# Repeating the queries of all batches on PE, with shared PSUM slots, split first loads and interleaved weights

## The chip, the cores and the metric

The kernel runs on one core of a Trainium2 chip. The metric is the device time of one execution in microseconds (us), and the median of several executions is quoted. The engines are PE (matmuls; PEld is its loading of weights), DVE (vector), ACT (scalar and activation), POOL (general) and SP, which here only issues DMA transfers. All quoted times come from the chip.

For a program on one core, a run is called slow when it is over 1.5% above the fastest run of the same kernel.

## The reference, cut to what matters

A polynomial-sketch attention over 4 batches, 4 heads, 1088 tokens and head size 32 feeds a feed-forward block with a squared relu:

```python
def phi(x):                                   # x: (batch, head, token, 32)
    a = einsum('rd,bhsd->bhsr', S1, x)        # 8 values
    b = einsum('rd,bhsd->bhsr', S2, x)        # 8 values
    return outer(a, b)                        # 64 features per token
q_p, k_p = phi(q), phi(k)
kv  = einsum('bhsf,bhsd->bhfd', k_p, v)       # one 64 x 32 matrix per head
z   = sum(k_p, axis=tokens)
x   = einsum('bhsf,bhfd->bhsd', q_p, kv) / (q_p @ z + 1e-6)
# x becomes 4352 tokens x 128
h = x @ w_in                                  # 128 -> 2048
out = relu(h) ** 2 @ w_out                    # 2048 -> 128
```

The disputed step is the product of query features. For every token the 8 values `a` and the 8 values `b` have to be spread over 64 partitions each before they can be multiplied element by element. This spreading is called "repetition" below.

## The kernel before: the parts that matter

The kernel describes its work as a graph of operations. Each one carries estimated costs for the engines that could run it. While the program is being built, a list scheduler picks an order, and the operations are then given to the engines in exactly that order. An engine takes its instructions in that order, so a wait in the middle of its list holds up everything behind it.

```python
G = Graph({"h": 2, "o": 1, "a": 3, "r": 4, "g": 4, "osb": 3})
h_t = [P(f"h{i}", [128, 1024]) for i in range(2)]     # PSUM, 1024 columns each
o_t = [P(f"o{i}", [128, 512]) for i in range(1)]
a_t = [P(f"a{i}", [128, 512]) for i in range(3)]      # for the attention
```

Batch 0 repeats its queries on PE: a matmul with a matrix that holds the sketch, repeated, writes the 64 copies directly. The others compute the sketch once (`qs`), and DMA makes the copies:

```python
if b == 0:
    for g in range(3):                                 # thirds of the tokens
        c0, n = 384 * g, 384 if g < 2 else 320
        # for x in (0, 1), for pr in (0, 1):
        nc.tensor.matmul(h_t[hb.slot][:, 512 * pr : 512 * pr + n],
                         SR[64 * pr : 64 * pr + 64, x].rearrange("p a x y -> p (a x y)"),
                         qT[i][64 * pr : 64 * pr + 64, c0 : c0 + n], start=True, stop=True)
        # ... ACT copies one factor to Ar, DVE multiplies the other by it
else:
    # ... qs = sketch of q (PE, ACT); bd = half of it written to DRAM
    reps.append(add(f"rb{b}.{pr}.{hp}", {"SP": (0.5, 4.0)}, f_rb, ...))   # Br <- bd, repeated
    reps.append(add(f"ra{b}.{ch}.{pr}", {"SP": (0.5, 4.0)}, f_ra, ...))   # Ar <- qs, repeated
    # ...
    o = add(f"qp{b}.{g}.{pr}", {"POOL": pool(n)}, f_qp, reps[...] + ...)  # qp = Ar * Br on POOL
# ... (cut)
o_num = add(f"num{b}.{g}", {"PE": pe(0.8)}, f_num, need + o_kve, vt(8 + g), alloc=[nb])
```

The pair `(0.5, 4.0)` is what the scheduler believes about one such transfer: 0.5 us to issue, landed 4.0 us after its start. The feed-forward block has two alternatives for the relu:

```python
o2 = add(f"r.{n}.{m}", {"ACT": act(W * N), "DVE": dve(W * N)}, f_r, [o1], p - 0.5, alloc=[rb], uses=[hb])
```

Of the kernel before, what the change touches and what calls it, by code (L numbers as in the profile page):

```python
# [16 lines left out]
LOOK = 0.12  # L17


class Buf:  # L20
    def __init__(self, kind):
        self.kind = kind
        self.users = []
        self.slot = None
        self.pending = 0


class Op:
    def __init__(self, name, alts, fn, deps, pri, alloc, uses, port):
        self.name, self.alts, self.fn, self.pri = name, alts, fn, pri  # L30
        self.deps = [d for d in deps if d is not None]
        self.alloc, self.uses, self.port = alloc, uses, port
        self.start = self.end = self.eng = None


class Graph:





# [4 lines left out]
    def add(self, name, alts, fn, deps=(), pri=0.0, alloc=(), uses=(), port=()):  # L46
        op = Op(name, alts, fn, deps, pri, list(alloc), list(alloc) + list(uses), port)
        for b in op.uses:
            b.users.append(op)
            b.pending += 1  # L50
        self.ops.append(op)
        return op

    def slot_time(self, kind):
        best = None
        for i, (t, b) in enumerate(self.slots[kind]):
            if b is not None and b.pending:
                continue
            if best is None or t < best[0]:
                best = (t, i)  # L60
        return best

    def run(self):
        eng_free, port_free = {}, 0.0
        todo = {id(o): len(o.deps) for o in self.ops}
        succ = {}
        for o in self.ops:
            for d in o.deps:
                succ.setdefault(id(d), []).append(o)
        ready = [o for o in self.ops if todo[id(o)] == 0]  # L70
        order = []
        while ready:
            cands = []
            for o in ready:
                t_slot = 0.0
                ok = True
                for b in o.alloc:
                    s = self.slot_time(b.kind)
                    if s is None:
                        ok = False  # L80
                        break
                    t_slot = max(t_slot, s[0] + SEM)
# [3 lines left out]
                for e, (busy, lat) in o.alts.items():  # L86
                    t = max(eng_free.get(e, 0.0), t_slot)
                    for d in o.deps:
                        t = max(t, d.end + (SEM if d.eng != e else 0.0))
                    if e in o.port:  # L90
                        t = max(t, port_free)
                    if best is None or t + lat < best[0]:
                        best = (t + lat, t, e, busy, lat)
# [4 lines left out]
                (c for c in cands if c[0] <= t0 + LOOK), key=lambda c: (c[1].pri, c[0]))  # L98
            for b in o.alloc:
                i = self.slot_time(b.kind)[1]  # L100
                b.slot = i
                self.slots[b.kind][i] = [t, b]
            o.start, o.end, o.eng = t, t + lat, e
            eng_free[e] = t + busy
            if e in o.port:
                port_free = t + busy
            for b in o.uses:
                b.pending -= 1
                sl = self.slots[b.kind][b.slot]
# [12 lines left out]
def act(n):  # L122
    return (0.833e-3 * n + 0.16, 0.833e-3 * n + 0.2)
# [6 lines left out]
def pool(n, rate=2.2e-3):  # L130
# [8 lines left out]
def kernel(  # L139
# [20 lines left out]
    HS = S // 2  # L160
# [3 lines left out]
    dr = ctx.enter_context(tc.tile_pool(name="dr", bufs=1, space=bass.MemoryType.DRAM))  # L164
# [8 lines left out]
    G = Graph({"h": 2, "o": 1, "a": 3, "r": 4, "g": 4, "osb": 3})  # L173
    h_t = [P(f"h{i}", [128, 1024]) for i in range(2)]
    o_t = [P(f"o{i}", [128, 512]) for i in range(1)]
    a_t = [P(f"a{i}", [128, 512]) for i in range(3)]
    r_t = [T(f"r{i}", [128, 1024], BF16) for i in range(4)]
    g_t = [T(f"g{i}", [128, 1024], BF16) for i in range(4)]
    osb_t = [T(f"osb{i}", [128, 512]) for i in range(3)]
# [5 lines left out]
    ST = T("ST", [128, 32])  # L185
    SK = T("SK", [128, 2, H, R])
# [4 lines left out]
    NB = 2  # L191
# [5 lines left out]
    vtl = [T(f"vtl{i}", [128, H, D]) for i in range(NB)]  # L197
# [4 lines left out]
    qs = [T(f"qs{i}", [128, HS]) for i in range(NB)]  # L202
    Ar = [T(f"Ar{i}", [128, 2, S]) for i in range(NB)]
    Br = [T(f"Br{i}", [128, 2, S]) for i in range(NB)]
    qp = [T(f"qp{i}", [128, 2, S]) for i in range(NB)]
    bd = [dr.tile([32, S], F32, name=f"bd{i}", tag=f"bd{i}") for i in range(NB)]
    den = [T(f"den{i}", [128, 12]) for i in range(NB)]
    rec = [T(f"rec{i}", [128, 12]) for i in range(NB)]
    xs = [T(f"xs{i}", [128, 3, 128], BF16) for i in range(NB)]

    add = G.add


    def f_S(eng):
        nc.vector.memset(S_sb, 0.0)
    o_S0 = add("S0", {"DVE": dve(32)}, f_S, pri=-100)

    def f_Sld(S, off):
        def f(eng):
            for h in range(H):  # L220
                nc.scalar.dma_start(out=S_sb[32 * h + off : 32 * h + off + R, :], in_=S)
        return f
    o_S1 = add("S1", {"ACT": (1.0, 3.0)}, f_Sld(S1, 0), [o_S0], -100)
    o_S2 = add("S2", {"ACT": (1.0, 3.0)}, f_Sld(S2, R), [o_S0], -100)
    o_SKz = add("SKz", {"DVE": dve(64)}, lambda e: nc.vector.memset(SK, 0.0), pri=-99)
    o_ST = add("ST", {"DVE": dve(32)}, lambda e: nc.vector.transpose(ST, S_sb), [o_S1, o_S2], -98)

    def f_SK(h):
        def f(eng):
            nc.vector.tensor_copy(  # L230
                SK[32 * h : 32 * h + 32, :, h, :],
                ST[32 * h : 32 * h + 32, 0 : 2 * R].rearrange("d (x r) -> d x r", x=2))
        return f
    o_SK = [add(f"SK{h}", {"DVE": dve(16)}, f_SK(h), [o_ST, o_SKz], -97) for h in range(H)]

    o_SRz = add("SRz", {"POOL": (0.4, 0.5)}, lambda e: nc.gpsimd.memset(SR, 0.0), pri=-99)
    o_SR = []
    for h in range(H):
        for x in range(2):
            def f(e, h=h, x=x):  # L240
                s = ST[32 * h : 32 * h + 32, R * x : R * x + R]
                s = s[:, None, :] if x else s[:, :, None]
                nc.gpsimd.tensor_copy(SR[32 * h : 32 * h + 32, x, h % 2], s.to_broadcast([32, R, R]))
            o_SR.append(add(f"SR{h}{x}", {"POOL": (0.2, 0.25)}, f, [o_ST, o_SRz], -96))

    o_iota = add("iota", {"POOL": (0.4, 0.5)}, lambda e: nc.gpsimd.iota(
        iot, pattern=[[1, 128]], base=0, channel_multiplier=-1), pri=-100)
    o_id = add("ident", {"DVE": dve(128)}, lambda e: nc.vector.tensor_single_scalar(
        ident, iot, 0, op=ALU.is_equal), [o_iota], 1)
    o_win = add("w_in", {"POOL": (1.2, 8.0)}, lambda e: nc.gpsimd.dma_start(  # L250
        out=w_in, in_=moe_w_in), pri=-99)
    o_wout = add("w_out", {"POOL": (1.2, 9.0)}, lambda e: nc.gpsimd.dma_start(
        out=w_out, in_=moe_w_out.rearrange("(ct c) d -> c ct d", c=128)), pri=-98)
    z_ops = {}
    for i in range(NB):
        def f_z(e, i=i):
            nc.gpsimd.memset(vp[i], 1.0)
            nc.gpsimd.memset(vp[i][64:128, :, NJ - 1, :], 0.0)
            nc.gpsimd.memset(kvz[i], 0.0)
        z_ops[i] = add(f"z{i}", {"POOL": (1.5, 1.6)}, f_z, pri=-97 + 50 * i)  # L260


# [6 lines left out]
    def attention(b, vt):  # L269
# [3 lines left out]
        def ld(dst, src, lo, hi):  # L273
            def f(e):
                nc.sync.dma_start(
                    out=dst[:, lo * D : hi * D],
                    in_=src[b].rearrange("h (t c) d -> (h t) (c d)", c=C)[:, lo * D : hi * D])
            return f
        parts = [(0, C)]
        o_k = add(f"ldk{b}", {"SP": (0.6, 3.4)}, ld(kin[i], k, 0, C), prev(b, "tk"), vt(0) - 30)  # L280
        o_q = add(f"ldq{b}", {"SP": (0.6, 3.4)}, ld(qin[i], q, 0, C), prev(b, "tq"), vt(0) - 29)
        o_v = []
        for g in range(4):
            def f(e, g=g):
                nc.sync.dma_start(
                    out=vin[i][32 * g : 32 * g + 32].rearrange("p h j d -> p h (j d)"),
                    in_=v[b].rearrange("h (t c) d -> t h c d", c=C)[:, :, 8 * g : 8 * g + 8, :].rearrange(
                        "t h c d -> t h (c d)"))
            o_v.append(add(f"ldv{b}.{g}", {"SP": (0.5, 3.0)}, f, prev(b, "vp"), vt(0) - 28))
        for g in range(2):  # L290
            def f(e, g=g):
                nc.sync.dma_start(
                    out=vtl[i][32 * g : 32 * g + 32],
                    in_=v[b].rearrange("h (t c) d -> t h c d", c=C)[:, :, 32 + g, :])
            o_v.append(add(f"ldv{b}.{4+g}", {"SP": (0.5, 3.0)}, f, prev(b, "vp"), vt(0) - 28))

        def f_vp(e):
            nc.gpsimd.tensor_copy(vp[i][:, :, 0:8, 0:D], vin[i])  # L298
            nc.gpsimd.tensor_copy(vp[i][0:64, :, 8, 0:D], vtl[i][0:64])
        o_vp = add(f"vp{b}", {"POOL": (1.6, 1.7)}, f_vp, o_v + [z_ops[i]] + prev(b, "kv"), vt(1))  # L300
        mine("vp", o_vp)


        kT3 = kT[i].rearrange("p (c t) -> p c t", t=32)
        prods = []
        for part, (j0, j1) in enumerate(((0, 4), (4, 9))):
            nj = j1 - j0

# [315 lines left out]
```

## Time and profile before

| Before, profiled run | |
|---|---|
| Median | 148.48 us |
| Span in the profile | 144.6 us |
| First feed-forward matmul | 27.8 us |
| PE stopped before numerator matmuls | 42.6 to 49.0 and 99.6 to 108.4 us |
| Time per chunk of 512 tokens at the end | 9.0 us |

The profile page of the kernel before gives busy time per engine, then rows of 40 equal slices of the span (3.6 us each) with the busy share in tenths. PEclk is the granted PE clock and DMA the busy share of the DMA engines, also in tenths:

```profile
PE 106.7 (74%) x1507; PEld 58.8 (41%) x1524; DVE 101.9 (70%) x192; ACT 67.7 (47%) x90; POOL 30.2 (21%) x48
...
PE   0008999799970496998999999995018898999850
...
PEclk9999999999999559999999999999555999999997
DMA  4999998788866687421300405896640003003042
...
L464 POOL TENSOR_TENSOR qp<-Ar,Br 128x384 f32<-128x384 f32 (+1 forms) x18 | 17.5, 998 | 54.7 <-DMA out_dram<-osb 36.7
L483 PE MATMUL a<-kvz,qp 128*32 128x66 f32 x576 | 13.8, 252 | 16.5 <-POOL qp L464 15.0
L539 DVE TENSOR_SCALAR r<-h 128x1024 bf16<-128x1024 f32 x13 | 15.8, 1218 | 3.6 <-PE h L531 3.6
```

No engine is busy throughout, and the average of 74% hides the interesting part. The PE row shows two holes, `04` and `01`, each with slices of about half rate in and behind it in the PEclk row. The groups (busy us, mean ns | idle before, releaser) name the waiter of the holes: the numerator matmuls L483 waited 15.0 us for POOL's product `qp`. The table by stages (window, length, busy us of each engine, granted clock, DMA share, GB/s) puts numbers on the holes:

```profile
42.60:49.00 6.40, 0.36 (x12) 0.20 (x14) 1.47 (x5) 0.39 (x1) 2.08 (x3) 0.85 0.65 177
49.00:55.00 6.00, 5.53 (x141) 3.94 (x146) 2.16 (x7) 0.55 (x2) 3.46 (x4) 0.59 0.81 141
99.60:108.40 8.80, 0.70 (x10) 0.20 (x8) 0.00 (x0) 0.62 (x1) 2.00 (x3) 0.62 0.52 153
118.00:140.00 22.00, 19.80 (x97) 9.20 (x95) 20.42 (x29) 14.40 (x15) 0.00 (x0) 1.00 0.18 31
```

In 15.2 us PE worked 1.06 us, and right after the first hole its clock was 0.59. The last row is the end, where only feed-forward is left: DVE is busy 20.42 of 22 us and ACT only 14.40, because DVE does the squares and also some of the relus (L539).

What did POOL wait for? The waits view of the kernel before says this (waiter, releaser: us, times, longest):

```profile
POOL qp L464 <- DMA out_dram<-osb: 36.7, 2, 34.4
...
PE a L483 <- POOL qp L464: 15.0, 6, 5.3
```

The first of these lines is a trap: a product of queries does not wait for a store of the output. The profile infers releasers from semaphores and names the one that came last. The chain of waits (start us, us, what) is the better witness for the first hole:

```profile
40.09 6.35 DMA Br<-bd
46.44 1.48 issue
47.91 1.00 POOL qp L464
48.96 1.33 PE a L483 x40
```

The repetition by DMA took 6.35 us where the scheduler's constant says 4.0. The scheduler had placed the numerators where it thought their data would be ready, and the feed-forward work behind them could not pass. For the second hole this view again names a store of the output. By the timeline, SP issued that batch's last copies `Ar` and `Br` only between 92.34 and 100.07 us, behind stores, and the first product on POOL ran at 104.10.

### The profile page before, as it was taken

To read this page: it belongs to the slowest core of one execution; us is meant where nothing else is said; L and a number is where in the kernel's file an instruction comes from. 1 tells how busy PE (TensorE), PEld (TensorE's weight loads), DVE (VectorE), ACT (ScalarE), POOL (GpSimd) and SP (SyncE) were. 2 spreads that over 40 slices of the span, in tenths; PEclk is the share of its full clock that TensorE was granted. 3 is DMA by queue.
4 is the path that set the end of the run, shared out by engine and by line. 5 is a ranking of instruction groups with operands and counts; after the bars stand their busy time and mean duration, and the time that the engine had idled before them with its cause. 6 is when DMAs were issued, how large, how long until landed. Compare 5 with 4: busy or idle time off the path is not lost.

```text
span 144.6 us, 3697 instructions
## 1 busy us (share of the span) xinstructions
PE 106.7 (74%) x1507; PEld 58.8 (41%) x1524; DVE 101.9 (70%) x192; ACT 67.7 (47%) x90; POOL 30.2 (21%) x48
## 2 busy tenths in 40 slices
PE   0008999799970496998999999995018898999850
PEld 0007477364520364565445437331006443333540
DVE  1219789898991038969999998693002999998960
ACT  0201331668580007643896896555000678377730
POOL 8308230300402750049200000000139000000000
PEclk9999999999999559999999999999555999999997
DMA  4999998788866687421300405896640003003042
GB/s 127 292 194 306 303 349 151 247 225 119 174 178 195 107 141 185 148 118 27 57 0 9 70 0 86 118 139 161 204 97 0 5 2 65 8 7 66 5 71 38
DMA packets 28017, 17.32 MB, mean 120 GB/s; under 512 B 22304, under 2 KB 24352, under 8 KB 28000
## 3 DMA queue, kind: packets, MB, share of 16 engines
q1 hardware_dynamic: 25664, 16.02, 47.2%
q0 software_dynamic: 2208, 1.05, 5.6%
q8 instruction: 12, 0.20, 0.5%
q10 hardware_dynamic: 128, 0.01, 0.1%
q14 instruction: 5, 0.04, 0.1%
HBM read 12.13 MB, written 2.65 MB: 102 GB/s over the span
## 4 chain that ended last, share of the span: by engine, by line
DVE 31%; PE 23%; SPq 15%; DMA 14%; issue 8%; POOL 1%; ACT 1%; POOLq 1%; DVEq 0%; ACTq 0%
DVE g L543 13%; SPq L451 7%; DMA S_sb<-in_S_dram 6%; PE o L550 6%; SPq L444 5%; PE h L531 5%; DMA Br<-bd 4%; DMA out_dram<-osb 4%; DVE r L539 4%; PE a L483 4%; SPq L566 3%; PE h L396 3%; DVE osb L557 3%; DVE xs L495 2%; PE a L359 2%
## 5 line engine op out<-in xcount | busy, mean ns | idle before, releaser
L537 ACT ACTIVATE r<-h 128x1024 bf16<-128x1024 f32 x55 | 54.6, 1023 | 21.7 <-PE h L531 16.2
L543 DVE TENSOR_TENSOR g<-r 128x1024 bf16<-128x1024 bf16 x68 | 45.2, 706 | 1.8 <-ACT r L537 1.1
L531 PE MATMUL h<-xT,w_in 128*128 128x512 bf16 (+1 forms) x135 | 38.8, 373 | 1.7 <-DVE r L539 0.4
L550 PE MATMUL o<-g,w_out 128*128 128x512 bf16 (+1 forms) x136 | 37.7, 367 | 2.5 <-DVE g L543 1.3
L464 POOL TENSOR_TENSOR qp<-Ar,Br 128x384 f32<-128x384 f32 (+1 forms) x18 | 17.5, 998 | 54.7 <-DMA out_dram<-osb 36.7
L483 PE MATMUL a<-kvz,qp 128*32 128x66 f32 x576 | 13.8, 252 | 16.5 <-POOL qp L464 15.0
L531 PEld LDWEIGHTS <-w_in 128*128 128x128 bf16 x144 | 13.5, 98 | 18.1 <-issue 5.0
L550 PEld LDWEIGHTS <-w_out 128*128 128x128 bf16 x144 | 12.8, 97 | 16.9 <-issue 7.2
L483 PEld LDWEIGHTS a<-kvz,qp 128*32 128x32 f32 x576 | 11.2, 128 | 20.8 <-POOL qp L464 17.8
L539 DVE TENSOR_SCALAR r<-h 128x1024 bf16<-128x1024 f32 x13 | 15.8, 1218 | 3.6 <-PE h L531 3.6
L493 DVE TENSOR_SCALAR den<-a 128x12 f32<-128x12 f32 x12 | 2.0, 164 | 20.6 <-PE a L483 20.6
L326 PE MATMUL a<-SK,kT 128*32 128x64 f32 x288 | 7.3, 251 | 11.5 <-DVE SK L230 11.5
L513 ACT COPY xT<-a 128x384 bf16<-128x384 bf16 (+1 forms) x10 | 4.6, 463 | 17.0 <-PE a L506 17.0
L326 PEld LDWEIGHTS a<-SK,kT 128*32 128x32 f32 x288 | 6.1, 129 | 13.8 <-DVE SK L230 11.5
L334 ACT COPY ka<-a 128x128 f32<-128x128 f32 (+1 forms) x8 | 2.2, 279 | 19.2 <-PE a L326 19.2
L342 DVE TENSOR_TENSOR kp<-a,ka 128x1024 f32<-128x1024 f32 (+1 forms) x8 | 10.7, 1341 | 0.0
L359 PEld LDWEIGHTS a<-vp,kp 128*64 128x64 f32 x288 | 9.0, 138 | 3.5 <-issue 2.3
L359 PE MATMUL a<-vp,kp 128*64 128x33 f32 x288 | 9.9, 224 | 0.3
L313 DVE STREAM_TRANSPOSE kT<-kin 128x128 f32<-128x128 f32 x32 | 7.0, 277 | 3.7 <-DMA kin<-in_k_dram 3.7
L298 POOL COPY vp<-vin 128x1024 f32<-128x1024 f32 x4 | 4.2, 1040 | 20.1 <-PE a L359 10.7
L495 DVE TENSOR_TENSOR xs<-a,rec 128x384 bf16<-128x384 f32 x12 | 6.7, 558 | 0.5
L557 DVE STREAM_TRANSPOSE osb<-o 128x512 f32<-128x512 f32 (+1 forms) x9 | 6.1, 675 | 0.9 <-PE o L550 0.7
(34 smaller groups left out, 51.4 us busy)
## 6 DMA issues: line engine op xcount, KB each, us to landing
Ar<-qs SPq DMA_DIRECT2D x12, 272.0 KB
Br<-bd SPq DMA_DIRECT2D x12, 272.0 KB
kin<-in_k_dram SPq DMA_DIRECT2D x4, 544.0 KB
qin<-in_q_dram SPq DMA_DIRECT2D x4, 544.0 KB
vin<-in_v_dram SPq DMA_DIRECT2D x16, 128.0 KB
out_dram<-osb SPq DMA_DIRECT2D x20, 64.0 KB
w_in<-in_moe_w_in_dram POOLq DMA_DIRECT2D x1, 512.0 KB, 7.9
w_out<-in_moe_w_out_dram POOLq DMA_DIRECT2D x1, 512.0 KB, 12.2
```

The costliest lines, as they stand in the source:

```text
L326: nc.tensor.matmul(o[32 * g : 32 * g + 32, :, j - j0, :], kT3[:, c, :], SK.rearrange("p x h r -> p x (h r)"), start=True, stop=True)
L342: nc.vector.tensor_tensor(out=kp[i][:, j0:j1].rearrange("p j h (x y) -> p (j h) x y", y=R), in0=bb[:, :, None, :].to_broadcast([128, m, R, ...
L359: nc.tensor.matmul(t[64 * (h % 2) : 64 * (h % 2) + 64, 33 * (h // 2) : 33 * (h // 2) + 33], kp[i][:, j, h, :], vp[i][:, h, j, :], start=(j ...
L451: nc.sync.dma_start(out=Ar[i][:, pr, HS * ch : HS * ch + HS], in_=qs[i][p0 : p0 + 16, None, :].to_broadcast([16, R, HS]))
L464: en.tensor_tensor(out=qp[i][:, pr, sl], in0=Ar[i][:, pr, sl], in1=Br[i][:, pr, sl], op=ALU.mult)
L483: nc.tensor.matmul(t[32 * cc : 32 * cc + 32, x, 2 * pr : 2 * pr + 2, :], qp[i][:, pr, 32 * c : 32 * c + 32], kvz[i][:, pr], start=True, st ...
L531: nc.tensor.matmul(h_t[hb.slot][:, N * w : N * w + N], w_in[:, 128 * ct : 128 * ct + 128], xT[:, n0 : n0 + N], start=True, stop=True)
L537: nc.scalar.activation(r_t[rb.slot], h_t[hb.slot], ACTF.Relu)
L539: nc.vector.tensor_scalar_max(r_t[rb.slot], h_t[hb.slot], 0.0)
L543: nc.vector.tensor_tensor(out=g_t[gb.slot], in0=r_t[rb.slot], in1=r_t[rb.slot], op=ALU.mult)
L550: nc.tensor.matmul(o_t[ob.slot][:, 0:N], w_out[:, ct, :], g_t[gb.slot][:, N * w : N * w + N], start=(ct == 0), stop=(ct == CT - 1))
L557: nc.vector.transpose(osb_t[sbuf.slot][:, 0:N], o_t[ob.slot][:, 0:N])
```

## The change

The intent is to take the repetition away from DMA altogether and to fill the time that opens up. It has five parts, and the diff shows at least two more that the short description does not mention.

1. All batches repeat on PE; DVE multiplies instead of POOL.
2. PSUM is given as three slots of 1024 columns that feed-forward and attention share, instead of two plus three small ones.
3. The first loads are split and reordered, and the two sketch loads need two transfers instead of eight.
4. The weights are loaded in parts, interleaved by four: one column block is read with a step of four.
5. The scheduler's model now knows of eight DMA lanes and of a shared DMA pipe.
6. Not mentioned: the chunks are 384, seven times 512, 384 instead of eight times 512 and 256.
7. Not mentioned: the relu on DVE carries a penalty of 0.6 us in the schedule, which steers it to ACT.

```diff
-    G = Graph({"h": 2, "o": 1, "a": 3, "r": 4, "g": 4, "osb": 3})
+    NH, NA, NR, NB = 3, 1, 4, 2
+    G = Graph({"h": NH, "o": 1, "a": NA, "r": NR, "g": NR, "osb": 3, "den": 3, "A": 2})
@@ weights @@
-        out=w_out, in_=moe_w_out.rearrange("(ct c) d -> c ct d", c=128)), pri=-98)
+    wo_src = moe_w_out.rearrange("(G c e) d -> c G (e d)", c=128, e=E)
+    for lo, hi in ((0, 1), (1, 2), (2, 4)):
+            nc.gpsimd.dma_start(out=w_in[:, 512 * lo : 512 * hi], in_=moe_w_in[:, 512 * lo : 512 * hi])
...
@@ first loads @@
-        o_k = add(f"ldk{b}", {"SP": (0.6, 3.4)}, ld(kin[i], k, 0, C), prev(b, "tk"), vt(0) - 30)
+        KS = ((0, 16), (16, 34)) if b == 0 else ((0, 34),)
+        QS = ((0, 12), (12, 34)) if b == 0 else ((0, 34),)
+            o_q.append(add(f"ldq{b}.{c0}", {"SP": (0.4, 3.4)}, ld(qin[i], q, c0, c1), prev(b, "tq"),
+                           vt(0) - 28.5 + c0 / 4, dma=1.6 * (c1 - c0) / 34, after=after))
...
@@ repetition @@
-        if b == 0:
-            for g in range(3):        # ... on PE
-        else:                         # ... qs, bd, Ar, Br by DMA, qp on POOL
+        for g in range(3):            # on PE, for every batch
+            o_ac = add(f"qa{b}.{g}", {"ACT": act(2 * n)}, f_ac, [ms[0]], ..., alloc=[sA], uses=[hA])
+            o = add(f"qp{b}.{g}", {"DVE": dve(2 * n, fix=0.16)}, f_qp, [ms[1], o_ac] + prev(b, "num"), ...)
@@ numerators may take an h slot @@
-            nb, tb = Buf("a"), Buf("a")
+            nb, tb, db = Buf("a", "h"), Buf("a", "h"), Buf("den")
...
@@ feed-forward @@
-                    nc.tensor.matmul(h_t[hb.slot][:, N * w : N * w + N], w_in[:, 128 * ct : 128 * ct + 128],
+                        w_in[:, 512 * (ct // E) : 512 * (ct // E) + 512].rearrange("p (c e) -> p e c", e=E)[:, ct % E],
-            o2 = add(f"r.{n}.{m}", {"ACT": act(W * N), "DVE": dve(W * N)}, f_r, ...)
+            o2 = add(f"r.{n}.{m}", {"ACT": act(W * N), "DVE": dve(W * N, fix=0.16) + (0.6,)}, f_r, ...)
```

## The prediction

> **What bounds the kernel now.** No single engine does. The profile page has PE busy 74%, DVE 70%, ACT 47% of 144.6 us. By the table of stages:
> - 0 to 11.4 us: PE does nothing. The small loads of S1 and S2 (eight DMAs) end only at 10.2 us; the timeline shows the first feed-forward matmul at 27.8 us.
> - 42.6 to 49.0 us and 99.6 to 108.4 us: PE works 0.36 and 0.70 us, DVE 1.5 and 0. The waits view shows PE's numerator matmuls behind POOL's qp product, which waits for the DMAs that replicate qs (Ar, Br). These waits sit mid-queue in front of feed-forward work, so everything stops.
> - After each stall the granted clock is about 0.6 for 4 to 6 us. The Trainium skill ("TensorE: Matmul & The Clock Gate", Part 1) says that an idle window of about 3.4 us halves the clock; this trace agrees.
> - 118 to 140 us: feed-forward only; output transposes come at 119.45, 128.15, 137.38, so about 9.0 us a chunk. DVE is busy 20.4 of 22 (eight squares of about 0.6, about three relus of 1.22, a transpose); ACT 14.4. Two h slots make the schedule give relus to DVE. PE needs only 32 x 0.215 = 6.9 us.
>
> **What the change does.**
> Removes: both DMA stalls (15.2 us less 1.1 us of work) and the slow-clock stages after them (estimate 4 us), all on the critical path. POOL's qp (17.5 us) goes too, which also sat on it.
> Start: two S loads instead of eight, K and Q halves first. I expect the first PE work near 5 us, the first feed-forward matmul at 14 to 17 us. That is an 11 to 13 us earlier start, but about 7 us of PE work that was done before 27.8 us is then still to do.
> Adds, for three batches: qr on PE, 0.72 us for each x and third (timeline), 4.2 us a batch, less the old qsk at 1.4: net 8.5 us PE. qp on DVE, 0.96+0.96+0.82: 8.2 us. qa on ACT 2.3 us a batch, less qs 0.8: net 4.6 us.
> PSUM: the third h slot lets ACT take more relus in the feed-forward stage: 9.0 to about 7.5 us a chunk over the last 2 to 3 chunks: 3 us. But the attention now borrows h slots from the feed-forward: loss of 3 to 5 us by waits on slots.
> Weights interleaved by four: larger w_out runs in the DMA, strided weight loads. Loads are 98 ns against 215 ns matmuls, hidden unless they more than double. Neutral.
>
> **Sum.** PE's own work is an estimate of 104 us (272 x 0.215 feed-forward, 12.6+4.2 qr, 5.7 key sketches, 10 kv, 9.6 numerators, 4 transposes), about 7 of it before feed-forward starts at 15. The rest, 97 us, at 91% (the 55 to 99.6 stage is PE busy 94%, with gaps inside) takes 107 us, plus the 4.5 us tail: span 126 to 127. Run times are about 3 us above the span here: about 129 us.
>
> Predicted 129 us, 8 in 10 between 121 and 137. Faster by over 2%: 0.95; within 2%: 0.03; slower: 0.02.
>
> **What would show it.** No PE gap over 3 us after 15 us and full granted clock; no Ar/Br DMA; first feed-forward matmul at 14 to 17 us; POOL almost idle; PE busy over 85% of the span; ACT busy up to 85 to 90 us; waits left over are PE on h slots (relu, qp) and DVE on ACT.
>
> **What would make it wrong.** First loads that contend with weights, so feed-forward starts after 20 us; attention holding two of three h slots, which drains the feed-forward pipeline for over 2 us at each qr/qp pair; strided weight loads doubling; DVE becoming the limit (about 94 us without relus) where the schedule bunches attention.

## The result, and the profile after

| | Before | After |
|---|---|---|
| Median of 4 runs | 148.48 us | 132.69 us |
| Lowest and highest | 147.61, 151.64 | 131.36, 136.39 |
| Span, granted clock of the profiled run | 144.6, 0.934 | 130.5, 0.979 |
| First feed-forward matmul | 27.8 us | 22.55 us |

The ratio is 0.890, with a 95% interval of 0.881 to 0.898. Here and below a ratio is the mean time of one kernel's fast runs over that of the other's of the same rounds, so it is not quite the ratio of the quoted medians. The change is faster, 3.7 us above the point predicted and inside the predicted range.

The page of the kernel after (slices of 3.26 us):

```profile
PE 115.0 (88%) x1572; PEld 62.2 (48%) x1572; DVE 96.6 (74%) x170; ACT 81.6 (63%) x108; POOL 11.1 (9%) x30
...
PE   0279599599999899999999999999999999999930
...
PEclk9999959999999999999999999999999999999996
DMA  1999999996700210220130001301300040031402
...
q8 instruction: 12, 0.20, 0.6%
...
L536 ACT ACTIVATE r<-h 128x1024 bf16<-128x1024 f32 (+1 forms) x72 | 65.6, 1026 | 19.7 <-PE h L527 19.5
...
L527 PEld LDWEIGHTS <-w_in 128*128 128x128 bf16 x144 | 15.1, 114 | 15.7 <-issue 4.5
```

The holes of the middle are gone, the clock row is full but for the sixth slice and the last, and no relu runs on DVE: all 72 are in the ACT group. What is left of holes lies in the first 30 us. The table by stages shows the same:

```profile
5.60:15.40 9.80, 7.84 (x152) 5.64 (x152) 5.86 (x7) 4.07 (x8) 3.63 (x7) 1.00 0.99 229
15.40:22.50 7.10, 7.06 (x147) 4.21 (x147) 4.39 (x8) 2.28 (x5) 0.00 (x0) 0.76 1.12 259
22.50:30.00 7.50, 5.71 (x123) 3.62 (x116) 6.30 (x15) 4.22 (x7) 1.68 (x4) 1.00 0.99 231
30.00:106.00 76.00, 75.53 (x1074) 39.69 (x1075) 61.67 (x107) 52.67 (x68) 4.31 (x8) 1.00 0.17 35
106.00:124.30 18.30, 17.84 (x84) 8.70 (x83) 15.11 (x24) 18.30 (x22) 0.00 (x0) 1.00 0.24 42
```

From 30 to 106 us PE is busy 75.53 of 76.00 us. At the end ACT is busy 18.30 of 18.30: the limit of that stage has moved from DVE to ACT. Its chunks now take 7.2 us instead of 9.0, from the output transposes at 112.96 and 120.14 (the chunk before still shares its time with attention, and the last, at 125.53, is a smaller one).

The start is worse than predicted. The timeline of the kernel after (start us, us, engine, operation, and in brackets the idle time before it and its releaser) shows two reasons:

```profile
5.59 1.08 PE L379 MATMUL a<-SK,kT 128*32 128x64 f32 x32 [5.59 <-DVE kT L365]
...
8.56 2.93 PE L447 MATMUL h<-qT,SR 64*128 64x384 f32 x8
...
14.47 0.91 DVE L434 STREAM_TRANSPOSE qT<-qin 128x704 f32<-128x704 f32 x1 [1.91 <-DMA qin<-in_q_dram]
...
15.31 0.18 DVE L425 COPY kvz<-a 64x66 f32<-64x66 f32 x1
...
15.44 1.43 PE L447 MATMUL h<-qT,SR 64*128 64x384 f32 x4 [1.35 <-DVE qT L434]
...
22.55 0.51 PE L527 MATMUL h<-xT,w_in 128*128 128x384 bf16 x2
23.00 0.90 PE L477 MATMUL h<-kvz,qp 128*32 128x66 f32 x48
25.45 0.33 PE L500 MATMUL h<-ident,xs 128*128 128x128 bf16 x3 [1.55 <-DVE rec L488]
```

First, DVE waited until 14.47 us for the second part of batch 0's queries. The small copy `kvz`, which all numerators need, stood behind that transpose in DVE's list and so came at 15.31. The numerators began at 16.80.

Second, PE stopped before 25.45 us. The bracket blames a `rec` that ended at 25.26, but that one belongs to the next group. The transposes read `xs`, done at 23.79, and the first of their weight loads had run at 23.84. In u_weights, which has the same order, the same `rec` was done at 22.34 and PE stood until 25.04. This stop turned out to be something else, as the experiments show.

### The profile page after: what moved, and what is told of

It reads as the page before. It is cut to its first block, busy times and chain, and to the rows that moved or that the text cites. A ratio compares the mean times of both kernels' runs of the same rounds, so it can differ in the third digit from the quotient of the medians.

```text
span 130.5 us, 3742 instructions
## 1 busy us (share of the span) xinstructions
PE 115.0 (88%) x1572; PEld 62.2 (48%) x1572; DVE 96.6 (74%) x170; ACT 81.6 (63%) x108; POOL 11.1 (9%) x30
## 4 chain that ended last, share of the span: by engine, by line
PE 70%; DMA 9%; DVE 7%; ACT 6%; issue 2%; ACTq 2%; DVEq 0%
PE o L550 21%; PE h L527 18%; PE h L447 14%; ACT r L536 6%; PE a L412 5%; DMA qin<-in_q_dram 5%; PE a L477 4%; DMA vin<-in_v_dram 4%; PE h L477 3%; DVE g L543 3%; PE a L379 2%; DVE osb L557 2%; PE h L500 1%; PE h L379 1%; ACTq L227 1%
## 5 line engine op out<-in xcount | busy, mean ns | idle before, releaser
L536 ACT ACTIVATE r<-h 128x1024 bf16<-128x1024 f32 (+1 forms) x72 | 65.6, 1026 | 19.7 <-PE h L527 19.5
L543 DVE TENSOR_TENSOR g<-r 128x1024 bf16<-128x1024 bf16 (+1 forms) x72 | 46.8, 662 | 11.3 <-ACT r L536 10.7
L447 PE MATMUL h<-qT,SR 64*128 64x384 f32 (+1 forms) x96 | 22.3, 560 | 1.3 <-DVE qT L434 1.3
L527 PEld LDWEIGHTS <-w_in 128*128 128x128 bf16 x144 | 15.1, 114 | 15.7 <-issue 4.5
L460 DVE TENSOR_TENSOR qp<-h,A 128x768 f32<-128x768 f32 (+1 forms) x12 | 10.9, 907 | 5.7 <-PE h L447 5.1
L456 ACT COPY A<-h 128x768 f32<-128x768 f32 (+1 forms) x12 | 9.2, 763 | 7.5 <-PE h L447 7.5
L447 PEld LDWEIGHTS h<-qT,SR 64*128 64x128 f32 x96 | 8.3, 202 | 9.0 <-issue 4.3
L365 DVE STREAM_TRANSPOSE kT<-kin 128x1088 f32<-128x1088 f32 (+2 forms) x5 | 5.4, 1073 | 3.0 <-DMA kin<-in_k_dram 3.0
L434 DVE STREAM_TRANSPOSE qT<-qin 128x384 f32<-128x384 f32 (+1 forms) x8 | 5.9, 734 | 2.0 <-DMA qin<-in_q_dram 1.9
L477 PE MATMUL h<-kvz,qp 128*32 128x66 f32 x288 | 6.1, 238 | 0.0
L477 PEld LDWEIGHTS a<-kvz,qp 128*32 128x32 f32 x288 | 4.4, 109 | 2.5 <-issue 1.3
```

Source lines behind the costliest of these rows:

```text
L447: nc.tensor.matmul(at(hb)[:, 512 * pr : 512 * pr + n], SR[64 * pr : 64 * pr + 64, x].rearrange("p a x y -> p (a x y)"), qT[i][64 * pr : 64 ...
L456: nc.scalar.copy(at(sA)[:, :, 0:n], at(hA).rearrange("p (m s) -> p m s", m=2)[:, :, 0:n])
L460: nc.vector.tensor_tensor(out=qp[i][:, :, c0 : c0 + n], in0=at(hB).rearrange("p (m s) -> p m s", m=2)[:, :, 0:n], in1=at(sA)[:, :, 0:n], o ...
L477: nc.tensor.matmul(t[32 * cc : 32 * cc + 32, x, 2 * pr : 2 * pr + 2, :], qp[i][:, pr, 32 * c : 32 * c + 32], kvz[i][:, pr], start=True, st ...
L527: nc.tensor.matmul(at(hb)[:, step * w : step * w + N], w_in[:, 512 * (ct // E) : 512 * (ct // E) + 512].rearrange("p (c e) -> p e c", e=E) ...
L536: nc.scalar.activation(o, view(at(hb)), ACTF.Relu)
```

## The experiments

Twelve kernels ran, in four jobs on four chips. Chips differ, so a kernel is compared with the kernel before, which ran in the same rounds. The kernel after was measured twice, but not in jobs 3 and 4, so t_late, t_late_hol, u_split and t_late_split are compared with it across chips. The fast runs of the kernel before average 148.36, 146.98, 148.41 and 147.16 us in jobs 1 to 4: part of a difference between ratios of different jobs, up to 1%, comes from this denominator. So I also give the means of the fast runs, which are 132.24 us (three runs) and 132.34 us (five) for the kernel after. None of the kernels gave a wrong result. The profiled runs of u_weights, f_hol, t_late and u_split count as slow by the 1.5% rule; from them I read only the order of events and where PE stops, and the times come from the fast runs.

| Kernel | Median us (runs) | Ratio to before, 95% | Job |
|---|---|---|---|
| after, first measurement | 132.69 (4) | 0.890 (0.881 to 0.898) | – |
| o_pe | 136.33 (4) | 0.920 (0.908 to 0.931) | 1 |
| u_dma | 152.84 (4) | 1.028 (1.017 to 1.040) | 1 |
| u_psum | 135.41 (4) | 0.911 (0.898 to 0.924) | 1 |
| u_weights | 131.68 (4) | 0.877 (0.864 to 0.890) | 1 |
| a_again (after, unchanged) | 132.63 (6) | 0.903 (0.894 to 0.911) | 2 |
| f_q1 | 131.16 (6) | 0.895 (0.887 to 0.903) | 2 |
| f_hol | 130.39 (6) | none | 2 |
| u_relu | 132.12 (6) | 0.901 (0.892 to 0.910) | 2 |
| t_late | 130.20 (6) | 0.874 (0.868 to 0.879) | 3 |
| t_late_hol | 129.20 (6) | 0.869 (0.865 to 0.874) | 3 |
| u_split | 130.26 (6) | 0.875 (0.870 to 0.881) | 3 |
| t_late_split | 127.89 (6) | 0.868 (0.864 to 0.872) | 4 |

### Only the repetition on PE: o_pe

My theory was that the stalls behind the DMA repetition were on the critical path and nearly the whole gain. The rival was that the gain comes mostly from the start and from PSUM. This kernel is the kernel before with one part of the change:

```diff
-        if b == 0:
+        if True:
             for g in range(3):        # repetition on PE
...
-            [ms[0]], vt(3 + g), uses=[hA])
+            [ms[0]] + prev(b, "qp"), vt(3 + g), uses=[hA])
-            [ms[1], o_ac], vt(6.5 + g), uses=[hB])
+            [ms[1], o_ac] + prev(b, "num"), vt(6.5 + g), uses=[hB])
```

> The kernel before with one part of the change alone: the queries of all four batches repeated on PE; loads, PSUM (two h slots, three a slots) and weights as before. Theory (the two DMA stalls were the main cost): no PE gap over 3 us after 15 us, 148.5 falls by the stalls (14 us) and the slow-clock stages (4 us) less the added PE work (8.5 us), so to about 137 to 140 us. Rival (the third h slot is what makes the repetition on PE pay, since a pair of repeated halves takes both of two h slots and drains the feed-forward): it stays above 144 us, with PE waiting on h slots at each pair.

It took 136.33 us. The means of the fast runs are 136.46 against 148.36, so this part alone is worth 11.9 us. The page of o_pe shows both holes gone and no slow slice but the last:

```profile
PE   0006999799999989999999999999998989899850
...
PEclk9999999999999999999999999999999999999996
```

The mechanism of the prediction is confirmed, and the rival falls. The start of o_pe is not better (first feed-forward matmul at 31.05 us), so the gain lies in the middle. The other 4 us from o_pe to the kernel after are not split up by these runs.

### Everything but the repetition on PE: u_dma

The opposite experiment takes the kernel after and gives batches 1 to 3 their DMA repetition and POOL product back.

```diff
+        if b == 0:
             for g in range(3):        # repetition on PE, as in after
+        else:
+            # qs, bd, Ar, Br by DMA and qp on POOL, as in before
```

> The kernel after with that part alone undone: batches 1 to 3 repeated by DMA again, the rest of the change kept. The schedule that the kernel computes while it is built plans 116.2 us for this one and 123.7 for the kernel after. Theory: the DMA stalls come back, at two or three places, PE idle 6 to 9 us each, and the time is 143 us or more, at least 8% above the kernel after. Rival (the early loads were what the replication collided with, and reordered loads clear the way for it): 134 us or less.

It took 152.84 us, slower than the kernel before: the interval of the ratio lies wholly above 1, but not wholly above 1.02. From u_dma to the kernel after is 20 us, and from before to o_pe it is 12 us, for the same part. So the parts of this change do not add up: without the repetition on PE, the rest of the change makes things worse. The page of u_dma has three holes instead of two, each with a slow clock behind it:

```profile
PE   0397982999930178994099999999601899999950
...
PEclk9999999599997559999857999999975589999997
```

The waits view of u_dma adds them up:

```profile
PE a L538 <- POOL qp L520: 24.2, 6, 6.6
```

That wait was 15.0 us in the kernel before. A schedule that is tight everywhere else relies more on the optimistic constant of 4.0 us, and loses more when the transfer is late. That last sentence is my reading; no run changes the constant alone.

### PSUM: u_psum

```diff
-    NH, NA, NR, NB = 3, 1, 4, 2
+    NH, NA, NR, NB = 2, 3, 4, 2
```

> The kernel after with PSUM alone undone: two h slots and three a slots, instead of three and one. The kernel's own schedule plans 126.4 against 123.7 us. Theory (PE is the limit from 30 to 104 us and gains nothing there from a third slot; the feed-forward stage at the end is limited by ACT's relus and needs the third slot little): 2 to 4 us slower, 135 to 137 us, lost in the repetition pairs. Rival (third slot is the main gain of the end stage): over 5 us slower, and the last feed-forward chunks take 9 us again instead of 7.3.

It took 135.41 us, a ratio of 0.911 against 0.890 and 0.903 in the two measurements of the kernel after. By the fast means that is 135.08 against 132.2 to 132.3 us, so the third slot seems worth 1 to 3 us, less than the 2 to 4 expected; the intervals overlap, and no view shows the loss in the repetition pairs. The rival, that the third slot makes the whole difference at the end, falls: with two slots the chunks at the end take 7.7 us (output transposes at 105.85, 113.69 and 121.38), still far from the 9.0 of before.

### Weights: u_weights

```diff
-    wo_src = moe_w_out.rearrange("(G c e) d -> c G (e d)", c=128, e=E)
-    wo_dst = w_out.rearrange("c (G e) d -> c G (e d)", e=E)
+    wo_src = moe_w_out.rearrange("(ct c) d -> c ct d", c=128)
+    wo_dst = w_out
-    w_in[:, 512 * (ct // E) : 512 * (ct // E) + 512].rearrange("p (c e) -> p e c", e=E)[:, ct % E]
+    w_in[:, 128 * ct : 128 * ct + 128]
```

> The kernel after with the interleave alone undone: w_in columns contiguous for a weight load, w_out rows of 512 B. The order of instructions stays the same. Theory: weight loads of w_in fall from 114 to 98 ns, hidden behind 215 ns matmuls; the weights' DMA takes more packets; within 1% of the kernel after. Rival (strided loads cost PE time): 2 us faster or more. Other rival (the short rows delay the first feed-forward): over 1.5 us slower, first feed-forward matmul after 24 us.

It took 131.68 us, with four runs between 129.61 and 132.94, of which only two count as fast. These two average 130.08 us, 2.2 us under the kernel after; all four average 131.48 against 133.28 (first measurement) and 132.55 (a_again). So the effect of the interleave is not settled to better than 1 or 2%: nothing suggests that it pays, and the first rival (2 us faster without it) is not excluded. The second rival falls: the first feed-forward matmul came at 19.64 us. The group of weight loads is clear (compare the 114 ns of the kernel after):

```profile
L527 PEld LDWEIGHTS <-w_in 128*128 128x128 bf16 x144 | 13.0, 98 | 16.7 <-issue 4.6
```

The step of four costs 16 ns per load, which stays hidden while PE is busy all through 30 to 106 us.

This kernel's profile brought a surprise, seen in the timeline of its PE. In the middle of the start, PE stood still for 4.07 us with nothing to wait for:

```profile
20.07 0.90 PE L477 MATMUL h<-kvz,qp 128*32 128x66 f32 x48
25.04 0.38 PE L500 MATMUL h<-ident,xs 128*128 128x128 bf16 x3 [4.07 <-issue]
```

### The late second part of the queries: f_q1 and f_hol, with a_again

In the start of the kernel after, I suspected the queue of DVE: `kvz` stands behind a transpose whose data come late. The late data have a cause of their own. SP came to the second part late, at 7.84 us, because loads of values stood in front of it, and these waited for earlier loads of values, as the waits of the kernel after on SP's queue show:

```profile
SPq L333 <- DMA vin<-in_v_dram: 4.8, 5, 1.6
```

f_q1 issues the second part right behind the first. f_hol leaves the load alone, but tells the schedule to put the transpose after `kvz`. a_again is the kernel after unchanged, for the same rounds.

```diff
 # f_q1
-                           vt(0) - 28.5 + c0 / 4, dma=...
+                           vt(0) - 28.5 + c0 / 100, dma=...
 # f_hol
+            if b == 0 and c0:
+                o.deps += o_kve
```

> The kernel after, unchanged, as the reference point on this chip for the three beside it: about 132.5 us. Theory: again the second part of the first queries lands at about 14.5 us and the first feed-forward matmul comes at 22 to 23 us, and there is an idle gap of PE of 1.5 us or more that ends near 25 us. If these do not repeat, they were accidents of one execution.

> The kernel after with one change: the second part of the first queries is issued right after the first part, ahead of the nine value loads (it was behind them and had to wait for a free DMA lane until 7.84 us). Theory (the late queries hold up DVE's in-order queue, so PE idles and the numerators start late): they land at 8 to 10 us, no PE wait on their transpose, first feed-forward matmul at 17 to 20 us, whole time 1.5 to 3 us less. Rival (the start is bound by how much PE work precedes the feed-forward, and the other loads slip by as much): within 1 us. If the PE gap that ends near 25 us follows the number of PE instructions (about 700) and not the transposes that stand there now, it appears again in front of other work.

> The kernel after with the order alone changed: the transpose of the second part of the first queries stands behind the two copies of kvz in the schedule, loads untouched. The queries still land at about 14.5 us. Theory (the cost was the head of the DVE queue, not the load itself): first numerators at about 14.4 instead of 16.8 us, first feed-forward matmul 2 us earlier, time 1 to 2 us less. Rival: PE work merely changes places and the time stays within 0.7 us.

f_q1 gained 1.1 us by the means of the fast runs (131.25 against 132.34), 0.8%, where 1.5 to 3 us were expected; the intervals of the two ratios overlap. Its data came in time (the transpose ran at 12.22 us without a wait), but its first feed-forward matmul came only at 21.30 us against 22.07 in a_again, and 17 to 20 were expected.

f_hol has no ratio, since one fast outlier of 127.84 us makes the rule call five of its six runs slow. The mean of all its runs is 130.08 us, against 132.55 for a_again on the same chip, so about 2.5 us were gained, with that caveat. The numerators of f_hol began at 13.86 us instead of 16.80 (15.75 in a_again), and `kvz` was copied at 13.34, ahead of the transpose at 13.48, which shows the blocked queue. But most of these 2 to 3 us were lost again before the first feed-forward matmul at 21.29 us, and then PE stopped. A caution on such single traces: u_relu and t_late have the start order of the kernel after, but no slow clock between 15.7 and 19.1 us, and their first feed-forward matmuls came at 20.69 and 20.14 us. So a difference of 2 us there can be the clock's and not the order's. The PE timeline of f_hol:

```profile
13.86 0.90 PE L479 MATMUL h<-kvz,qp 128*32 128x66 f32 x48 [0.63 <-ACT kvz L425]
...
23.29 0.31 PE L479 MATMUL h<-kvz,qp 128*32 128x66 f32 x4
25.82 0.89 PE L479 MATMUL h<-kvz,qp 128*32 128x66 f32 x44 [2.22 <-issue]
```

The PE timeline of f_q1 shows the same thing in another group:

```profile
23.18 0.63 PE L379 MATMUL h<-SK,kT 128*32 128x64 f32 x27
25.72 0.31 PE L379 MATMUL h<-SK,kT 128*32 128x64 f32 x5 [1.91 <-issue]
```

These groups are single operations of the graph, 48 and 32 matmul records with the same inputs and the same output. PE stopped inside them, after 4 of 48 and after 27 of 32. So data or a buffer can hardly be the reason. In three kernels with different orders the stop ended at nearly the same time, 25.04, 25.72 and 25.82 us.

### What stops PE in the middle of a group: instruction fetch

The traces record every DMA packet, those of the instruction queue too. The page of the kernel after counts 12 such packets with 0.20 MB (q8), so each holds about 16 KB. I counted the PE records (matmuls and weight loads) in the order of time, and found in the kernel after that from the fourth packet on, each starts within about 1 us of the time at which PE passes record 164 + 256k. The first three come late, by 2.9, 3.2 and 5.7 us, and they fall in the stage in which the loads keep the DMA engines at nearly 100%. The second packet matters for this stop. From the packet records and PE records of each trace ("at" is the start of the last record before the stop, so the idle time itself is 0.1 to 0.35 us shorter than the distance to "resumes"):

```
              PE passes   2nd packet   PE stops       at    resumes   resume minus
              record 420  starts       after record                  packet start
after            19.4       22.6          699        23.84   25.45       2.8
a_again          18.6       21.7          699        23.36   24.45       2.8
u_weights        16.0       22.6          699        20.93   25.04       2.4
u_dma            17.6       22.5          699        22.00   25.17       2.6
u_psum           19.6       22.5          700        24.04   24.94       2.5
u_relu           17.6       22.5          699        21.97   25.04       2.6
f_q1             18.8       23.1          699        23.59   25.72       2.7
f_hol            17.9       23.3          700        23.38   25.81       2.5
u_split          16.5       22.8          699        22.88   25.78       2.9
t_late           17.0       20.6          699        21.43   23.11       2.5
t_late_hol       17.7       20.4       (no stop over 0.3 us there)
t_late_split     17.8       19.3       (no stop over 0.3 us there)
```

In ten of these twelve traces, with different orders of work, PE stops after 699 or 700 records and resumes 2.4 to 2.9 us after the packet started. In the two others PE reached record 699 only at 23.08 and 23.95 us, 2.7 and 4.6 us after the packet, so no stop was due. In o_pe, with the loads of before, PE stood 0.8 us after record 701 and resumed 2.7 us after its second packet. Without the hold that follows, the packet starts at 21.7 to 23.3 us, whether PE passes record 420 at 16.0 or at 19.6, so the earlier PE reaches record 700, the longer it stands. An improvement of the start is partly eaten here; this took part of f_hol's gain.

The stop can cost more than its length. In u_weights, u_dma, u_relu, u_split and t_late the recorded clock went to 0.5 between 24.4 and 26.4 us, during the stop or within 1.3 us after it, for 3.4 us (6.8 in u_split). In the other five it stayed full.

The Trainium skill, page "Runtime: NRT & Kernel Launch", section "Instruction fetch mechanics", says that instructions are refilled in blocks of 16 KiB, 256 instructions, by a DMA queue of the sequencer itself, and that crossing a block is "mostly hidden". The packet size and the step of 256 in these traces agree. "Mostly hidden" does not hold for this one packet, which comes while the loads fill the DMA engines.

The table is a correlation, and the profile does not name such a wait: it writes "issue", or a false releaser as in the kernel after. So I tested it.

### Holding back loads that are not urgent: t_late and t_late_hol

If late packets are the cause, fewer loads at that time must bring the packet forward and shorten the stop. The loads of batches 2 and 3 are not needed so early. They are held back by an otherwise idle operation on POOL, which they wait for (it reads the first key buffer, so it fixes the order without taking away any wait):

```diff
+        if b == 1:
+            hist["hold"] = [add("hold", {"POOL": (0.1, 0.15)},
+                lambda e: nc.gpsimd.tensor_copy(gate, kin[0][:, 0:1]), o_vp, vt(6))]
 # and in every load of k, q and v:
-            prev(b, "tk")
+            prev(b, "tk") + hist.get("hold", [])
```

> The kernel after with one thing changed: the loads of batches 2 and 3 start only after batch 1's values have been copied on POOL (at about 24 us, instead of from 14.5 us), by an idle POOL copy that reads the key buffer which the first of these loads overwrites. Instruction order on PE unchanged. In seven traces so far PE stops after 699 or 700 matmul and weight-load records, wherever that falls in its work, and starts again [...]at 24.4 to 25.8 us. Theory (PE's instructions arrive late because the loads fill the DMA engines): the second packet starts 1 us or more earlier (by 21 us), the gap shrinks under 0.5 us, and the time falls by 0.5 to 2 us. Rival (the gap is a wait of the work itself): it stays, and the time is within 0.3 us.

> The same together with the order of the run in which the transpose of the late queries stands behind the copies of kvz. That run began its feed-forward earlier but lost it to the PE gap that ended at 25.8 us. Theory: without that gap the earlier start counts, 1.5 to 3 us less than the kernel after, 129.5 to 131 us, below each of the two changes alone. Rival (PE work bounds all of it): no better than the better of the two.

t_late has a ratio of 0.874 (0.868 to 0.879) against 0.903 (0.894 to 0.911) for a_again. By the means of the fast runs it is 129.69 against 132.34 us, 2.0%, on different chips. From 19.5 to 23 us the DMA share was 0.37 instead of 1.12 in the kernel after, and the second packet started at 20.6 us. The stop ended at 23.11 instead of about 25, but it did not shrink, and in this the expectation missed: PE was idle for 1.6 us, against 1.5 in the kernel after and 1.0 in a_again, because PE reached record 699 earlier too, at 21.43 us. The PE timeline of t_late:

```profile
20.59 0.90 PE L480 MATMUL h<-kvz,qp 128*32 128x66 f32 x48
23.11 0.33 PE L503 MATMUL h<-ident,xs 128*128 128x128 bf16 x3 [1.62 <-DVE rec L491]
```

t_late_hol, which adds f_hol's edit, has a ratio of 0.869, whose interval overlaps that of t_late: its packet started at 20.4 us, PE has no idle time above 0.5 us between 20 and 30 us, and its granted clock was 0.998 in the profiled run. The stop in t_late stands between the same two operations as in the kernel after, the numerators and the transposes behind them, so the work there is unchanged. The stop follows the packet and not the work, which supports the theory. How much of the time gained is the earlier packet, how much the full clock and how much the freer DMA engines, these runs do not separate.

### The first loads in one piece: u_split and t_late_split

The change splits batch 0's first loads to begin earlier. This kernel undoes that alone:

```diff
-        KS = ((0, 16), (16, 34)) if b == 0 else ((0, 34),)
+        KS = ((0, 34),)
-        QS = ((0, 12), (12, 34)) if b == 0 else ((0, 34),)
+        QS = ((0, 34),)
-        for a in range(2 if b == 0 else 1):
+        for a in range(1):                     # loads of v, whole
-        TS = ((0, 512), (512, S)) if b == 0 else ((0, S),)
+        TS = ((0, S),)
 # ... and the dependencies that go with it
```

> The kernel after with the split of the first loads undone: the keys, queries and values of batch 0 come whole, as for the other batches (S loads, the order of queues, the gate before the weights kept). Theory: the first transposed keys come about 1 us later than at 5.6 us, but the second part of the queries no longer lands late (all queries by 8 us), so the first feed-forward matmul is within 1 us of 22 us and the time within 1 us of the kernel after: the split brought little, since the start is held by the queue order and then by PE's instructions. Rival (the split is what makes the early start): 2 us slower or more.

> Two edits to the kernel after, together: the first loads come whole (the run before showed nothing lost by that) and the loads of batches 2 and 3 start only after batch 1's values are copied. Theory (PE's instructions were late behind the loads): the second instruction packet starts by 20.8 us instead of 22.8, PE's idle gap after about 700 records ends by 23.5 us or is gone, and the kernel takes 128 to 129.5 us, a ratio of 0.86 to 0.87 to before, against 0.8757 with whole loads alone. Rival: the gap stays at 25.8 us and the ratio is 0.875 or more.

u_split took 130.26 us, with a ratio of 0.875 (0.870 to 0.881), below both measurements of the kernel after (fast means 129.96 against 132.2 to 132.3 us, on different chips). The split, which I had counted as part of the early start, gains nothing and probably costs some 2 us. PE did begin later (7.74 us instead of 5.59), but fewer and larger loads had everything there sooner, and the first feed-forward matmul came at 20.50 us. Then the stop came. Here is the PE timeline of u_split (of a slow run of 132.71 us, so it shows where the stop falls and not what the fast runs lose by it):

```profile
20.50 0.84 PE L527 MATMUL h<-xT,w_in 128*128 128x384 bf16 x4
...
22.57 0.52 PE L379 MATMUL h<-SK,kT 128*32 128x64 f32 x18
25.78 0.65 PE L379 MATMUL h<-SK,kT 128*32 128x64 f32 x14 [2.68 <-issue]
```

It is in the middle of a group again.

t_late_split joins u_split and the hold. It took 127.89 us, with all six runs between 127.06 and 128.04, and a ratio of 0.868 (0.864 to 0.872). This is the best version: it beats before, and it beats after, whose lowest run of all was 131.26 us. Its packet started at 19.3 us. The same group of 32 now runs without a stop, as the PE timeline of t_late_split shows:

```profile
23.70 0.65 PE L382 MATMUL h<-SK,kT 128*32 128x64 f32 x32
```

Its page shows a full clock and fewer DMA-filled slices in the start:

```profile
PE   0049999899999999999999999999999999999930
...
PEclk9999999999999999999999999999999999999999
DMA  1999992999601200400300004002200040040403
```

How much of t_late_split's gain over u_split is the hold is less sure: the intervals of the ratios overlap, and the two ran on different chips.

### The relu's penalty: u_relu

```diff
-            "DVE": dve(W * N, fix=0.16) + (0.6,)}
+            "DVE": dve(W * N, fix=0.16)}
```

> The kernel after with the schedule's penalty of 0.6 us on relus given to DVE taken out again, as before: the schedule then gives 6 of 72 relus to DVE and plans 121.8 instead of 123.7 us. Theory (ACT limits the last 20 us at 0.914 us a relu, against 0.86 us of PE): the last three chunks shorten by some tenths of a us each, 0.5 to 1.5 us less in all. Rival (DVE's relu takes 1.22 us and stands in front of squares, so PE waits more in the mixed stage): the time grows by 1 us or more.

This was a miss. Without the penalty 6 of the 72 relus went to DVE, but the time did not change: 132.09 against 132.34 us by the means of the fast runs. The chunks at the end (output transposes at 105.86, 114.10, 120.48 and 125.11, the last a smaller one) took 8.2 and 6.4 us, 7.3 on average, about as in the kernel after. The relief of ACT at the end was real in the plan and did not show on the chip. There was little to win: PE's own 32 x 0.215 = 6.9 us a chunk leave 0.3 us of the 7.2, an estimate of 1 us over three chunks. This kernel also has the stop of PE at the start, 21.97 to 25.04 us, longer than the kernel after's.

## Why the prediction was right or wrong, point by point

**The stalls behind the DMA repetition: right, in cause and in size.** The prediction put "15.2 us less 1.1 us of work" and an estimated 4 us of slow clock on the critical path, against additions on PE of 8.5 us, so a net of 9.6 us. o_pe measured the net: 11.9 us. u_dma shows that this part is also the one on which the others depend.

**The clock: right for the stalls.** The prediction cites the Trainium skill, "TensorE: Matmul & The Clock Gate", Part 1, for an idle window of about 3.4 us. The granted clock was 0.59 to 0.62 around and after the stalls of before, and 1.00 in o_pe up to 132 us, where the stalls are gone. The halving agrees; the 3.4 us as an idle time does not come out of this trace: in the first stall the recorded clock fell 4.6 us after PE stopped (42.56 and 47.11 us), in the second 1.9 us (99.86 and 101.72). The forecast of a full clock after 15 us missed one stretch, 15.7 to 19.1 us.

**The start: wrong.** The step that failed is "the first feed-forward matmul at 14 to 17 us. That is an 11 to 13 us earlier start". It came at 22.55 us, 5.2 us earlier than in the kernel before. The first PE work did come "near 5 us", at 5.59. Four things fill the difference, and the first is close to what was named under what would make the prediction wrong (there, loads that contend with the weights):

- Loads contend. The second part of the queries was waited for until 14.47 us, because SP issued it behind the value loads, at 7.84 us, and it took 6.6 us to land while the DMA engines were 99% busy.
- Queues are in order. `kvz` stood behind that transpose; f_hol moved the numerators from 15.75 us (a_again, same chip) to 13.86 us by the order alone.
- PE was at half rate at the very start. In the kernel after, eight repetition matmuls took 2.93 us at 8.56 us. In u_weights these eight took 2.93 us at 8.31 us, and eight of the same shape 1.45 us at 15.22. The Trainium skill's page on the clock gate, Part 1, says that what is issued in the first 3.4 us or so of activity runs at half the clock; the halved speed agrees. It lasted longer, though: those matmuls ended at 11.49 us, 5.9 us after PE's first. The PEclk row reads 9 in these slices because the trace has no clock event before 12.29 us.
- After the wait for the queries the clock fell again: 0.76 in the stage from 15.40 to 22.50 us, and the numerators at 16.80 us took 1.55 us instead of 0.90. In u_relu, with the same order at the start and no such fall, the first feed-forward matmul came at 20.69 us: nearly 2 of the missing us are the clock's in this trace.

The stop by late instruction packets adds to this after the first feed-forward matmul: about 1.5 us in the kernel after, and up to 4.0 us in the others.

**The main stage: too pessimistic, which hid half of that miss.** The prediction took "97 us, at 91%", that is 107 us from the first feed-forward matmul to the tail. By the timeline it was 103.6 us (22.55 us to 126.1 us, the end of the last output transpose). PE was busy 99% of the 76 us in the middle. The error of the start, 5.5 to 8.5 us, was thus made smaller by about 3 us, and the span came out as 130.5 instead of 126 to 127. PE's own work was mis-sized as well: it was busy 115.0 us instead of 104, of which 15.0 instead of 7 before the first feed-forward matmul, in part at half rate. After it, PE was busy 100.0 us at 96% of the time, instead of 97 us at 91%. (The two measures are not quite the same: a single 128x512 matmul is recorded as 379 ns, while in a row they start 215 ns apart, which is what the estimate counts.) That errors of opposite sign met so near 129 us is luck.

**Run time above span: mis-sized.** The prediction added 3 us to the span. The runs show 1.7 us in the profiled run of the kernel after (132.24 against 130.5), and 1.7 to 2.2 us in the later ones.

**PSUM and the end: right in size, the cause not settled.** "9.0 to about 7.5 us a chunk" was measured as 7.2. The prediction put it down to the third slot. u_psum has only two slots and still needs only 7.7; it kept the relu penalty. u_relu has three slots and no penalty and averages 7.3. o_pe, which has neither, needs 8.6 (output transposes from 101.43 to 127.25). So either seems enough to get most of it, by one trace each, and both runs carry the rest of the change too. The penalty was in the diff and not in my sum. The predicted loss of "3 to 5 us by waits on slots" did not show: PE is busy 99% of the middle.

**Weights: not contradicted.** A load took 114 against 98 ns and stayed hidden in the middle. Whether the interleave is "neutral" in the whole time is open, since the two fast runs without it were 2.2 us faster.

**What would show it.** POOL is almost idle (9%), no repetition DMA is left, PE is busy 88% and ACT 81.6 us, where 85 to 90 us of ACT were predicted. No PE gap over 3 us occurs after 15 us in the kernel after.

## What to carry to other kernels

A transfer that sits between two engines' work in an in-order list costs what the list behind it is worth, so repeat data on an engine if it has room, and check the schedule's constants against the chain of waits. When an engine stops in the middle of a group of identical instructions, look at the instruction queue's packets: loads that are not urgent can delay them, and holding those loads back gave about 1 to 2% here, by means compared across chips. Loading the first data in smaller pieces starts work earlier but does not have to finish it earlier.

## What the Trainium skill lacked or had wrong

- "Runtime: NRT & Kernel Launch", section "Instruction fetch mechanics", calls the cost of crossing a 16 KiB block mostly hidden. In the ten traces named, PE was idle for 0.6 to 4.0 us after 699 or 700 records and resumed 2.4 to 2.9 us after the second packet of the queue had started. With loads held back the packet came 1.1 to 3.5 us earlier, and the stop was gone in two kernels and ended 1.3 to 2.3 us earlier, but no shorter, in t_late. The page does not say that data loads delay the refill. Why it is 700 records and not a multiple of 256 stays open.
- "TensorE: Matmul & The Clock Gate", Part 1, gives an idle window of about 3.4 us. The clock also fell to 0.55 (16.0 to 19.5 us of the kernel after) following an idle time of only 1.35 us, and did not fall in f_hol after 1.69 us of idle at 17.94 us. The page calls the window free-running. The recorded changes fit that: within each trace they lie whole multiples of 3.41 us apart (12.29, 15.70, 19.12 and 128.34 us in the kernel after). Why 1.35 us was enough in one window and 1.69 us was not stays open.
- The same page warns that the recorded clock events are not reliable. No run here shows a wrong event: matmuls took twice their time at 8.56 us, before the first recorded event at 12.29 us, and the PEclk row reads full where nothing is recorded.
- The same page, section "Weight-path perf modes — Fast Weight Load (FWL) and DoubleRow", gives no cost for weights read with a step. A step of four took 114 ns against 98 ns for a load without it.
